# Loading the first input block in full rows and doing its first stage whole, in the prologue of an FFT-and-MLP kernel

## The chip, the cores and the metric

The kernel runs on one core of one Trainium2 chip. The metric is the device time in microseconds (us). Lower is better. A *run* is one timed execution. Most executions of one kernel agree within 0.3%, and that is about the size of the effects here, so medians over five or six runs are given with their range, and ratios with a 95% interval. A *profile* is one execution with a trace. Its *span* runs from the first to the last instruction.

## The reference

```python
# x: (8, 3008, 256) fp32, filt_r and filt_i: (1505, 256), w_in: (256, 2048), w_out: (2048, 256)
X = np.fft.rfft(x, axis=1)
Y = X * (filt_r + 1j * filt_i)[None, :, :]
y = np.fft.irfft(Y, n=3008, axis=1)
h = y.reshape(24064, 256) @ w_in
out = np.maximum(0.01 * h, h) @ w_out
```

The Fourier transform along the sequence is split, 3008 = 94 x 32. Each of the 8 batch elements goes through stage S1 (one 94-point transform as a matmul for each of the 32 values of n2), 32x32 block transposes (T1), stage S2 (32-point transforms), the products with the two filters, the inverse of S2 ("sa"), transposes back (T2), and the inverse of S1 ("sb"). Then comes the MLP, called MoE in the code: 256 to 2048, leaky ReLU, back to 256.

## The kernel before

Batch elements 1 to 7 are transformed beside the MLP, which keeps TensorE busy. Only batch element 0 has nothing to hide behind. Its passage is the *prologue*. It is worked in halves of d (the 256 columns): the first half of x is loaded, then that half's filters, then the second half of x and its filters, and the stages of the two halves are interleaved by hand.

```python
def x_load(b, n0=0, nn=N2, d0=0, dn=D):      # rows of dn values, cast fp32 -> fp16
    ...                                      # issued from GpSimd (POOL)
for i in range(FP):                          # FP = 4, step = 8: the tables of S1
    nc.sync.dma_start(f1_sb[:, ts(i, step), :], f1_d.ap()[i])
nc.sync.dma_start(small_sb[:], small_d.ap())
for hf in range(2):
    for n0 in (0, N2 // 2):
        x_load(0, n0, N2 // 2, hf * DH, DH)  # 16 n2 of 128 columns
    filt_load(fa_sb, filt_r, hf * DH, DH)
    filt_load(fb_sb, filt_i, hf * DH, DH)
# ... (cut)
def first_s1(hf, g, kind, copy):             # 4 n2 of 128 columns: matmuls, one eviction
    ps = bank(kind, 4, DH)
    for j in range(4):
        n2 = 4 * g + j
        nc.tensor.matmul(ps[:, j, :], f1_sb[:N1, n2, :], x_sb[:N1, n2, ts(hf, DH)],
                         start=True, stop=True)
    spread(big[0], 4 * g, ps, copy, hf * DH // 2)

def upper(hf):                               # filters to the other 64 partitions
    for t, cp in ((fa_sb, act), (fb_sb, dve)):
        cp(t[64:P, :, ts(hf, DH)], t[0:64, :, ts(hf, DH)])

def keep_warm(n):                            # n matmuls whose result nobody reads
    ...
for g in range(8):
    first_s1(0, g, two[(g // 2) % 2], (act, dve)[g % 2])
t1_part(0, 0, True)(), t1_part(0, 1, True)()
upper(0)
first_s2(0, 8, 8, True)                      # True: products on POOL, from ACT's copy
first_s2(0, 0, 8, False)                     # False: products on VectorE (DVE)
first_s2(0, 20, 4, True)
first_s2(0, 16, 4, False)
for g in range(8):
    first_s1(1, g, two[g % 4 == 3], dve if g in (3, 5, 7) else act)
x_load(1)
t1_part(0, 2, True)(), t1_part(0, 3, True)()
upper(1)
first_sa(0, 0), first_sa(0, 16)              # inverse of S2, evicted by ScalarE (ACT)
first_s2(1, 8, 8, True)
first_s2(1, 0, 8, False)
# ... w_out load (cut)
first_sa(0, 8), first_sa(0, 20)
first_s2(1, 16, 8, False)
first_sa(1, 0)
first_t2(0), first_t2(1)
first_sa(1, 16), first_sa(1, 8)
first_t2(2), first_t2(3)
keep_warm(5)
for g in range(8):
    first_sb(g, act, two[(g // 2) % 2])
keep_warm(3)
for g in range(8, 16):
    first_sb(g, (act, dve)[g % 2], two[(g // 2) % 2])
```

## Time and profile before

| | kernel before |
|---|---|
| time, median of 3 runs (range) | 785.91 us (785.34 to 786.10) |
| time and span of the profiled execution | 787.67 us and 785.9 us |
| first MoE matmul in that profile | 45.56 us |
| length of the part after it | 740.34 us |

### The profile page before, as it was taken

Reading aid. Unit: us, or ns where it says so; the run is one execution under the profiler, and the core shown is the slowest. Engines: PE = TensorE matmul, PEld = TensorE weight load, DVE = VectorE, ACT = ScalarE, POOL = GpSimd, SP = SyncE. Lnnn points to the kernel's source line nnn. Section 1 sums busy time; section 2 is a strip of 40 time slices with the busy share of each in tenths; the row PEclk is TensorE's granted clock in tenths of the full one; section 3 lists DMA queues with packets and bytes.
Section 4 is the critical chain, followed back from the end, with each engine's and each line's share of the span. In section 5 each row is a group of like instructions: output and inputs, shape, how many; then the busy total and the mean of one; then the engine's idle time right before and its main releaser. Section 6 shows DMA issues by size and latency. Waiting matters only on the chain.

```text
span 785.9 us, 13623 instructions
## 1 busy us (share of the span) xinstructions
PE 763.0 (97%) x5812; PEld 528.6 (67%) x5812; DVE 365.1 (46%) x459; ACT 557.0 (71%) x794; POOL 150.7 (19%) x122
## 2 busy tenths in 40 slices
PE   2799999999999999999999999999999999999998
PEld 1356677666776677866777667776677667676666
DVE  3869760784327652387316754078432765200000
ACT  3686768676687767877687775967668776666664
POOL 5773400240003400052001410024000340000000
PEclk9999999999999999999999999999999999999999
DMA  9943010501032010501014101050100101101111
GB/s 174 214 59 94 28 42 28 122 28 41 28 79 70 28 41 28 119 31 41 28 41 108 41 28 41 28 120 28 42 28 28 41 28 42 41 28 41 41 41 54
DMA packets 42013, 43.39 MB, mean 55 GB/s; under 512 B 14274, under 2 KB 40514, under 8 KB 41282
## 3 DMA queue, kind: packets, MB, share of 16 engines
q0 software_dynamic: 15760, 16.99, 13.2%
q1 hardware_dynamic: 26192, 25.53, 9.3%
q8 instruction: 45, 0.74, 0.4%
q14 instruction: 16, 0.13, 0.1%
HBM read 34.10 MB, written 24.64 MB: 75 GB/s over the span
## 4 chain that ended last, share of the span: by engine, by line
PE 93%; ACT 2%; issue 1%; DVE 0%; ACTq 0%; DVEq 0%
PE po_ps L379 41%; PE ph L365 40%; PE pf L170 3%; PE pf L237 2%; PE pf L210 2%; PE pf L225 2%; PE pf L379 1%; ACT big L181 1%; ACT gt_c L370 1%; PE pf L284 1%; PE ph L260 0%; PE ph L301 0%; DVE fy_h_c L276 0%; PE po_ps L313 0%; PE pf L301 0%
## 5 line engine op out<-in xcount | busy, mean ns | idle before, releaser
L370 ACT ACTIVATE gt_c<-ph 128x1024 f16<-128x1024 f32 x376 | 384.8, 1024 | 194.8 <-PE ph L365 193.8
L365 PE MATMUL ph<-yt,w_in_sb 128*128 128x512 f16 (+7 forms) x1728 | 386.6, 351 | 0.4 <-ACT yt L304 0.2
L379 PE MATMUL po_ps<-w_out_sb,gt_c 128*128 128x256 f16 x2944 | 381.5, 272 | 0.6 <-ACT ost_c_t L386 0.6
L379 PEld LDWEIGHTS <-gt_c 128*128 128x128 f16 x3008 | 290.7, 98 | 86.7 <-issue 1.7
L365 PEld LDWEIGHTS <-w_in_sb 128*128 128x128 f16 x1728 | 163.0, 98 | 95.2 <-issue 1.0
L218 POOL TENSOR_TENSOR y_b_g<-p_b_g,p_b_g 128x512 f16<-128x512 f32 x84 | 106.9, 1273 | 225.5 <-DVE p_b_g L216 225.5
L181 ACT CAST big<-pf 128x512 f16<-128x512 f32 x195 | 111.8, 606 | 11.8 <-PE pf L251 11.7
L193 DVE STREAM_TRANSPOSE big<-big 128x1024 f32<-128x1024 f32 x32 | 55.8, 1846 | 127.1 <-ACT big L181 126.7
L240 DVE CAST yt<-pf 128x376 f16<-128x376 f32 x112 | 56.3, 545 | 85.9 <-PE pf L237 85.9
L214 DVE TENSOR_TENSOR p_b_g<-pf,fa_sb 128x512 f32<-128x512 f32 x84 | 58.1, 692 | 38.0 <-PE pf L210 35.5
L386 ACT COPY ost_c_t<-po_ps 128x256 f32<-128x256 f32 x184 | 69.4, 377 | 6.7 <-PE po_ps L379 5.6
L201 DVE STREAM_TRANSPOSE big<-big 128x1024 f32<-128x1024 f32 x28 | 51.1, 1936 | 34.5 <-ACT big L181 34.5
L215 DVE TENSOR_TENSOR p_b_g<-pf,fb_sb 64x512 f32<-64x512 f32 x84 | 58.2, 693 | 1.1
L216 DVE TENSOR_TENSOR p_b_g<-pf,fb_sb 64x512 f32<-64x512 f32 x84 | 57.4, 683 | 1.1
L132 POOL DMA_DIRECT2D x_sb<-in_x_dram x12 | 8.5, 713 | 256.6 <-PE pf L170 255.5
L237 PEld LDWEIGHTS <-big 128*128 128x128 f16 x448 | 25.7, 98 | 13.2
L170 PE MATMUL pf<-x_sb,f_sb 94*128 94x256 f16 x224 | 33.8, 272 | 0.1
L210 PE MATMUL pf<-big,small_sb 128*128 128x512 f16 x84 | 31.8, 379 | 0.0
L225 PE MATMUL pf<-y_b_g,small_sb 128*128 128x512 f16 x84 | 31.8, 379 | 0.0
L237 PE MATMUL pf<-i_sb,big 128*128 128x94 f16 x448 | 28.7, 206 | 0.0
L170 PEld LDWEIGHTS <-f_sb 94*128 94x128 f16 x224 | 21.0, 97 | 9.5 <-issue 1.3
L347 POOL TENSOR_SCALAR fb_sb<-fb_sb 64x6144 f16<-64x6144 f16 x1 | 15.7, 15742 | 0.4 <-DVE fy_h_c L276 0.4
(45 smaller groups left out, 142.8 us busy)
## 6 DMA issues: line engine op xcount, KB each, us to landing
out_dram<-ost_c_t SPq DMA_DIRECT2D x92, 256.0 KB, 2.1
x_sb<-in_x_dram POOLq DMA_DIRECT2D x6, 1536.0 KB, 11.3
x_sb<-in_x_dram POOLq DMA_DIRECT2D x4, 384.0 KB, 11.0
w_in_sb<-in_moe_w_in_dram POOLq DMA_DIRECT2D x1, 1024.0 KB, 14.9
w_out_sb<-in_moe_w_out_dram POOLq DMA_DIRECT2D x1, 1024.0 KB, 10.2
x_sb<-in_x_dram POOLq DMA_DIRECT2D x1, 1024.0 KB, 9.1
f_sb<-fwd_const SPq DMA_DIRECT2D x4, 192.0 KB, 3.2
fa_sb<-in_filt_r_dram POOLq DMA_DIRECT2D x4, 192.0 KB, 9.8
```

What stands on the lines that cost most here:

```text
L170: nc.tensor.matmul(ps[:, j, :], f1_sb[:N1, n2, :], x_sb[:N1, n2, :], start=True, stop=True)
L181: copy(paired(dst)[:, ds(n0, nn), ds(e0, de)], ps.rearrange("p n (e t) -> p n e t", t=2))
L214: nc.vector.tensor_tensor(p1[:], ps, fa, AL.mult)
L215: nc.vector.tensor_tensor(p2[0:64], ps[64:P], fb[64:P], AL.mult)
L216: nc.vector.tensor_tensor(p2[64:P], ps[0:64], fb[0:64], AL.mult)
L218: nc.gpsimd.tensor_tensor(y1[:], p1[:], p2[:], AL.add)
L237: nc.tensor.matmul(ps[:, j, :], src[:, dt, n2, :], i1_sb[:, n2, :], start=True, stop=True)
L240: copy(yv[:, :, ds(4 * h, 4)], ps.rearrange("p c a -> p a c"))
L365: nc.tensor.matmul(ph[:, j, ds(o, ln)], w_in_sb[:, dt, ts(ct, P)], yts[b % 2][:, dt, ds(lo, ln)], start=(dt == 0), stop=(dt == NDT - 1),)
L370: nc.scalar.activation(gts[ci][:, ds(2 * g, 2), :], ph, AF.Lrelu)
L379: nc.tensor.matmul(po, gts[ci][:, ct, ts(tj, P)], w_out_sb[:, ct, :], start=(ct == 0), stop=(ct == NCT - 1))
L386: nc.scalar.copy(ost[:, tj % 2, :], po)
```

## The change

The intent: load x in long rows, so that the transfer is more efficient; do S1 in one pass, so that no second pass sits in the middle of the prologue; split into halves of d only from T1 on; and put TensorE's work in the order in which its inputs become ready.

```diff
     nc.sync.dma_start(small_sb[:], small_d.ap())
+    for i in range(FP):
+        x_load(0, step * i, step)
     for hf in range(2):
-        for n0 in (0, N2 // 2):
-            x_load(0, n0, N2 // 2, hf * DH, DH)
         filt_load(fa_sb, filt_r, hf * DH, DH)
         filt_load(fb_sb, filt_i, hf * DH, DH)
 ... (cut)
-    def first_s1(hf, g, kind, copy):
-        ps = bank(kind, 4, DH)
-        for j in range(4):
-            n2 = 4 * g + j
-            nc.tensor.matmul(ps[:, j, :], f1_sb[:N1, n2, :], x_sb[:N1, n2, ts(hf, DH)],
+    def first_s1(n0, n, kind, copy):
+        ps = bank(kind, n, D)
+        for j in range(n):
+            nc.tensor.matmul(ps[:, j, :], f1_sb[:N1, n0 + j, :], x_sb[:N1, n0 + j, :],
                              start=True, stop=True)
-        spread(big[0], 4 * g, ps, copy, hf * DH // 2)
+        spread(big[0], n0, ps, copy)
 ... (cut)
-    for g in range(8):
-        first_s1(0, g, two[(g // 2) % 2], (act, dve)[g % 2])
+    for g in range(6):
+        first_s1(4 * g, 4, "ph", (dve, act)[g % 2])
+    for g in range(4):
+        first_s1(24 + 2 * g, 2, two[g == 3], (act, dve)[g % 2])
     t1_part(0, 0, True)(), t1_part(0, 1, True)()
     upper(0)
     first_s2(0, 8, 8, True)
+    x_load(1)
     first_s2(0, 0, 8, False)
+    t1_part(0, 2, True)()
     first_s2(0, 20, 4, True)
     first_s2(0, 16, 4, False)
-    for g in range(8):
-        first_s1(1, g, two[g % 4 == 3], dve if g in (3, 5, 7) else act)
-    x_load(1)
-    t1_part(0, 2, True)(), t1_part(0, 3, True)()
+    t1_part(0, 3, True)()
+    first_sa(0, 0), first_sa(0, 16)
     upper(1)
-    first_sa(0, 0), first_sa(0, 16)
     first_s2(1, 8, 8, True)
+    first_sa(0, 8), first_sa(0, 20)
     first_s2(1, 0, 8, False)
     nc.gpsimd.dma_start(w_out_sb[:], moe_w_out.rearrange("(ct p) d -> p ct d", p=P))
-    first_sa(0, 8), first_sa(0, 20)
     first_s2(1, 16, 8, False)
 ... (cut)
         first_sb(g, act, two[(g // 2) % 2])
-    keep_warm(3)
     for g in range(8, 16):
```

## The prediction

> **What bounds the kernel now.** I read the page first (busy shares, slices, chain), then the windows of the span cut at the first MoE matmul, then the timeline and the waits of the first 46 us, then the DMA view in short windows.
>
> From the page of the kernel before:
>
> ```profile
> PE 763.0 (97%) x5812; PEld 528.6 (67%) x5812; DVE 365.1 (46%) x459; ACT 557.0 (71%) x794; POOL 150.7 (19%) x122
> ...
> PE   2799999999999999999999999999999999999998
> ```
>
> From the windows, cut at 45.56 us (columns: stretch, length, then PE, PEld, DVE, ACT, POOL busy, clock, DMA share, GB/s):
>
> ```profile
> 0.00:45.56 45.56, 26.86 (x236) 16.03 (x237) 27.13 (x31) 26.38 (x42) 32.56 (x31) 0.96 1.27 187
> 45.56:785.90 740.34, 736.12 (x5576) 512.58 (x5575) 337.97 (x429) 530.62 (x752) 118.10 (x92) 1.00 0.17 47
> ```
>
> After 45.56 us TensorE is busy 736.1 of 740.3 us: nothing that the diff touches can shorten that part. Before it no engine is busy for more than 72%; it is a chain of dependent steps. So the time is 740.3 plus the prologue's length, and the change is about the prologue.
>
> The prologue's timeline (start, duration, engine, line, operation; in brackets idle time and what ended it):
>
> ```profile
> 9.59 1.01 PE L251 MATMUL pf<-x_sb,f_sb 94*128 94x128 f16 x8 [9.59 <-DMA x_sb<-in_x_dram]
> ...
> 12.45 1.01 PE L251 MATMUL pf<-x_sb,f_sb 94*128 94x128 f16 x8 [0.99 <-DMA x_sb<-in_x_dram]
> ...
> 15.15 2.37 DVE L193 STREAM_TRANSPOSE big<-big 128x1024 f32<-128x1024 f32 x2
> ...
> 22.46 1.46 PE L251 MATMUL pf<-x_sb,f_sb 94*128 94x128 f16 x12
> ...
> 26.88 2.37 DVE L193 STREAM_TRANSPOSE big<-big 128x1024 f32<-128x1024 f32 x2
> ...
> 34.70 1.22 DVE L276 TENSOR_TENSOR fy_h_c<-ph,fa_sb 128x1024 f16<-128x1024 f32 x1 [1.06 <-PE ph L260]
> ...
> 39.69 2.37 DVE L292 STREAM_TRANSPOSE big<-big 128x1024 f32<-128x1024 f32 x2 [0.35 <-ACT big L285]
> ...
> 45.56 1.28 PE L365 MATMUL ph<-yt,w_in_sb 128*128 128x512 f16 x4 [0.17 <-ACT yt L304]
> ```
>
> The reader is to see three clocks. Loads set the first 12.5 us. From 15.15 to 42.06 VectorE runs an almost closed sequence (27 us with some 4.7 us of gaps), in which the second half of d has its S1 only at 22.46 to 26.1, so that its transpose waits until 26.88. Then ScalarE's twelve copies of the last inverse stage (40.28 to 45.51) carry it to the MoE.
>
> The DMA view of 12 to 16 us (256 B packets, x and filters by halves), and of 27 to 29 us (4 KB packets, the first MoE weight):
>
> ```profile
> DMA packets 2865, 0.72 MB, mean 181 GB/s; under 512 B 2865, under 2 KB 2865, under 8 KB 2865
> ```
>
> ```profile
> DMA packets 100, 0.41 MB, mean 205 GB/s; under 512 B 0, under 2 KB 0, under 8 KB 100
> ```
>
> **What the Trainium skill says.** "DMA: Bandwidth & Descriptors", Specifications, wants at least 512 B per transfer for line rate, and its section on small descriptors names a fixed cost per packet. The trace agrees in direction only: 256 B packets land at 181 GB/s, 4 KB ones at 205, 13% more (both cast from fp32, so twice that is read). The same page, "Issuing engines are not separate DMA queues", says that all queues share 16 engines; the trace agrees, the tables loaded from SP and x from POOL share the 3 to 7 us stretch at 135 to 224 GB/s. "TensorE: Matmul & The Clock Gate", "What's actually happening", says that TensorE idles at 1.2 GHz and goes to 2.4 after a busy free-running window of about 3.4 us. The trace agrees: 512-column matmuls of L284 come every 0.43 us at 31 to 33 us and every 0.215 us after 34.4 us; the granted clock is 0.50 from 30.6 to 34.0 us. The same page gives run-to-run phase as a cause of variation.
>
> **The change part by part.**
>
> *Loads.* Total bytes are equal. First x goes from four loads of 1536 packets to four of 96 packets of 4 KB (8 n2 of 256 values). All of x now precedes all filters. Bytes of the tables: four of 192 KB and one of 96 KB, 885 KB; at 280 GB/s (DMA view, 2 to 3.5 us) and with 350 KB moved by 3.0 us (windows of 1 us: 51 and 299), 1.9 us are left when x starts, near 3.0 us. x: 1573 KB at 205 = 7.7 us. Last byte at 3.0+1.9+7.7 = 12.6, landing some 0.9 later: 13.5 us (estimate). Before, half of d was there at 12.4, so the first transpose does not start earlier: this is the price. First-half filters, 786 KB at 181 = 4.35 us, end at 16.95 and land near 18.9 (lags of about 1.9 us for such packets: the first x load landed at 9.55 when the windows' sum less the tables says 727 KB had moved, 393 of them its own). Before, the last of them was there by about 16.4.
>
> *S1.* 64 matmuls of 128 columns at 0.107 us become 32 of 256 at 0.213 cold: 6.8 us on TensorE either way, all of it under the load now. Evictions: before 16 of 512 columns (ACT 0.59, DVE 0.69), now six of 1024 (ACT 1.02 from L370's row, DVE 1.22 from L276's) and four of 512. Each quarter (1.9 us of arrival) has one DVE and one ACT eviction in parallel, so they keep up. The last quarter: 8 x 0.213 after 13.5 = 15.2, plus 0.1 and a DVE copy of 0.69: first transpose at 16.0 against 15.15. Loss 0.85 us.
>
> *The middle.* From the second half go 3.6 us of TensorE (22.46 to 26.05) and three DVE evictions (2.07 us) between the first multiplications and the second transposes. I add up the new DVE order with measured durations: transposes 16.0 to 18.4; wait for the filter, copy 0.95 until 19.85; S2 on PE 4 x 0.43 from 18.5, so multiplications 20.4 to 22.85 (2.45); third transpose to 24.05 (1.2); the pair of 0.69 to 25.4; fourth transpose to 26.6 (before: 29.25). So 2.65 us are gained here. Then the other engines: ACT's copies of the first half's inverse must wait for 25.4, end at 27.0; ACT copies fa 2.75 to 29.75, evicts 1.1 to 30.85 for POOL, which starts at 30.3 (31.21 before). PE: two S2 matmuls to 27.55, six inverse ones (2.6 us cold, 1.3 warm), two S2 matmuls: DVE's next multiplications start at 31.0 cold or 29.8 warm (31.29 before). So the new PE order takes 2.2 to 3.5 us of the gain back as a DVE gap. Two pairs of multiplications (4.9) end at 35.95 or 34.7; before 37.05. Gain here 1.1 to 2.35.
>
> *The end.* The last inverse matmuls on PE: 8 x 0.215 warm, then five warming ones 1.1, so the last stage starts at 37.6 (warm early) or 38.9 (warm from about 31 to 34 on); before 39.8. Its first eviction comes 0.48 later and the twelve ACT copies take 5.23 as before. Removing the three warming matmuls frees 0.75 us of PE (42.31 to 43.06), of which nearly nothing shows, as ACT copied until 43.39 and had 0.16 us of gap. First MoE matmul: 37.6+0.48+5.25 = 43.3, or 38.9+0.48+5.25 = 44.6. Middle 43.7, as the S1 burst may leave PE warm earlier than I count; against 45.56 a gain of 1.9 us. 740.3 + 43.7 = 784.0.
>
> **The rivals.**
> One: loads. If the filters in second place are what the first S2 products wait for, each us of their delay past 20 us goes through to the end. For it: the filters' share of the queue is unchanged and they move behind 1.57 MB instead of 0.79. Against: by my sum fb's upper copy ends at 19.85 and S2's matmuls at 20.35. If they land 2 us later: 786.
> Two: clock. Without a dense stretch of TensorE between 26 and 34 us, or without the three warming matmuls, the last inverse and the last stage run at half clock: 8 x 0.215 and 5 x 0.215 more, 2.8 us, and the first MoE slots too: 786.5 to 787.5. For it: the phase of the window is free. Against: PE has a closed stretch from 26.7 to 31.
> Three: DVE stays closed. If PE is warm through the middle (S1 at 8 x 0.213 of each 1.9 us is a 90% busy stretch), and the loads land 1 us sooner, DVE's gap shrinks: 781.5 to 782.5.
> Four: the freed prologue is given back in the first MoE slots by a late load. Against: the first MoE weight landed 14 us before use and the next x moves up, as POOL issues it before its second pair instead of after. I give it nearly nothing.
>
> **Range and chances.** My middle is 784.0. Rival three gives the low edge, 781.8; rivals one and two the high edge, 786.5. The prologue would have to lose 16 us of its 45 for "faster by over 2%", and grow by 16 for slower: 1% each. 98% within 2%.
>
> **What would show it right or wrong.** First MoE matmul near 43.7 (43.3 to 44.6), and the rest 740.3 long. Last x quarter at 13.5, first transpose at 16.0, fourth ended at 26.6. A DVE gap of 2 to 3.5 us before the multiplications of the second half, ended by PE. The twelve ACT copies still 5.2 us. Wrong if the first transpose is at 14.5 or 17.5, if filters end DVE's or ACT's waits after 20 us, if L284's matmuls after 35 us come every 0.43 us, or if the part after the prologue changes by over 0.5 us.

## More of the kernel before

The timeline of VectorE in the kernel before shows the second half of the work (start, length, engine, line, operation, output <- input; in brackets the idle time before the first of the group and what ended it):

```profile
29.29 0.96 DVE L308 COPY fb_sb<-fb_sb 64x3072 f16<-64x3072 f16 x1
31.29 1.23 DVE L276 TENSOR_TENSOR fy_h_c<-ph,fa_sb 128x1024 f16<-128x1024 f32 x1 [1.04 <-ACT fx_h_c L268]
...
36.97 2.36 DVE L292 STREAM_TRANSPOSE big<-big 128x1024 f32<-128x1024 f32 x2
```

After the filter copy VectorE waits 1.04 us for ScalarE, then multiplies, and the transposes back start at 36.97.

## The result, and the profile after

| | before | after |
|---|---|---|
| time, median of 6 runs (range) | 785.62 us (784.71 to 786.52) | 786.66 us (785.51 to 789.65) |
| ratio after/before, 95% interval | | 1.0021 (1.0000 to 1.0043) |
| time and span of the profiled execution | 787.67 and 785.9 us | 789.03 and 787.1 us |
| first MoE matmul in it | 45.56 us | 46.75 us |

A ratio is the mean time of one kernel's fast runs over that of the other's of the same rounds, so it is not quite the ratio of the medians. I predicted 784.0 us, at most 786.5. The change did not save 1.9 us; it cost about 1 us by the medians and 1.7 us by the means. The prediction was wrong.

Four views of the kernel after. First the page's busy times, to be held against those of before:

```profile
PE 764.4 (97%) x5777; PEld 526.2 (67%) x5777; DVE 366.2 (47%) x457; ACT 556.1 (71%) x790; POOL 148.8 (19%) x122
```

TensorE is busy 1.4 us longer, VectorE 1.1 us, ScalarE 0.9 us less: on this page the change is not to be seen, as it lies in who waits for whom. Then the windows, cut at the first MoE matmul, with the columns of the prediction:

```profile
0.00:46.75 46.75, 28.31 (x201) 13.62 (x202) 28.24 (x29) 25.51 (x38) 30.99 (x31) 0.96 1.09 182
46.75:787.10 740.35, 736.13 (x5576) 512.59 (x5575) 337.95 (x429) 530.61 (x752) 117.80 (x92) 1.00 0.17 47
```

The second part is 740.35 us against 740.34. Everything happens in the prologue, as predicted, and the difference of the two spans, 1.2 us, is the difference of the two prologues. The timeline of the prologue after:

```profile
9.03 1.86 PE L250 MATMUL ph<-x_sb,f_sb 94*128 94x256 f16 x8 [9.03 <-DMA x_sb<-in_x_dram]
...
18.21 2.37 DVE L193 STREAM_TRANSPOSE big<-big 128x1024 f32<-128x1024 f32 x2
...
27.31 1.23 DVE L193 STREAM_TRANSPOSE big<-big 128x1024 f32<-128x1024 f32 x1
...
32.31 1.22 DVE L275 TENSOR_TENSOR fy_h_c<-ph,fa_sb 128x1024 f16<-128x1024 f32 x1 [1.68 <-ACT fx_h_c L267]
...
40.61 2.37 DVE L291 STREAM_TRANSPOSE big<-big 128x1024 f32<-128x1024 f32 x2 [1.40 <-ACT big L284]
...
46.75 1.28 PE L364 MATMUL ph<-yt,w_in_sb 128*128 128x512 f16 x4 [0.17 <-ACT yt L303]
```

The reader is to see that the first transpose moved from 15.15 to 18.21, and that the fourth ends at 28.54 against 29.25 before: the whole loss of 3.06 us is made good in the middle, and 0.71 more. It is lost again after that. VectorE has a gap of 1.68 us before the second half's products, ended by ScalarE (before, that gap was 1.04), and one of 1.40 us before the last transposes (before, 0.35).

The second gap falls into a window of half clock. The windows of the kernel after around it, each 3.41 us long and cut at or one such length before a change in the record of the granted clock (the last three numbers are clock, DMA share and GB/s):

```profile
33.79:37.20 3.41, 1.70 (x8) 0.41 (x7) 3.41 (x4) 1.58 (x3) 3.41 (x4) 1.00 0.86 183
37.20:40.62 3.42, 3.42 (x10) 1.21 (x9) 2.02 (x3) 2.42 (x4) 3.34 (x2) 0.50 0.54 65
40.62:44.03 3.41, 3.32 (x79) 2.64 (x79) 2.36 (x2) 2.20 (x7) 3.41 (x1) 1.00 1.38 187
```

In the first window TensorE was busy for half of the time (1.70 us); in the next one the record grants half the clock, and ten matmuls took all of 37.20 to 40.62. The kernel before had the same in its profile (0.50 from 30.6 to 34.0, after a window with 2.08 us busy). How busy a window has to be does not come out of these traces: in "before, early S1" (below) one with only 1.78 us busy, 22.20 to 25.61, was followed by full clock. So neither of the two profiles that I had was of an undisturbed execution, and a comparison of the two mixes the change with luck.

### The profile page after: what moved, and what is told of

Same layout as the page of the kernel before. It is cut to its first block, busy times and chain, and to the rows that moved or that the text cites. A ratio compares the mean times of both kernels' runs of the same rounds, so it can differ in the third digit from the quotient of the medians.

```text
span 787.1 us, 13542 instructions
## 1 busy us (share of the span) xinstructions
PE 764.4 (97%) x5777; PEld 526.2 (67%) x5777; DVE 366.2 (47%) x457; ACT 556.1 (71%) x790; POOL 148.8 (19%) x122
## 4 chain that ended last, share of the span: by engine, by line
PE 94%; ACT 2%; DVE 1%; DMA 1%; issue 1%; POOL 0%; ACTq 0%; DVEq 0%; POOLq 0%
PE po_ps L378 41%; PE ph L364 40%; PE pf L170 3%; PE pf L237 2%; PE pf L225 2%; PE pf L210 2%; DMA x_sb<-in_x_dram 1%; PE pf L378 1%; ACT big L181 1%; DVE fy_h_c L275 1%; PE pf L283 1%; ACT gt_c L369 1%; PE ph L250 0%; ACT fa_sb L307 0%; DVE big L193 0%
## 5 line engine op out<-in xcount | busy, mean ns | idle before, releaser
L181 ACT CAST big<-pf 128x512 f16<-128x512 f32 x190 | 109.0, 607 | 0.0
L132 POOL DMA_DIRECT2D x_sb<-in_x_dram x12 | 6.6, 553 | 256.6 <-PE pf L170 255.8
L250 PE MATMUL ph<-x_sb,f_sb 94*128 94x256 f16 x26 | 6.2, 412 | 10.1 <-DMA x_sb<-in_x_dram 9.6
```

Of the source, the lines that this page charges most:

```text
L181: copy(paired(dst)[:, ds(n0, nn), ds(e0, de)], ps.rearrange("p n (e t) -> p n e t", t=2))
```

## The experiments

**How they are read.** Of every profile I note three numbers: the start of the first transpose ("T1 starts"), the first MoE matmul, and their difference, the *rest* of the prologue. The first is set by loads and S1, the rest by the chain of engines. The last column says whether a window of half clock fell into the rest of the prologue after the first release.

| kernel | last x needed lands | T1 starts | first MoE | rest | half-clock window |
|---|---|---|---|---|---|
| before, as profiled | 12.41 | 15.15 | 45.56 | 30.41 | yes |
| before with filling matmuls | 10.41 | 13.15 | 42.42 | 29.27 | no |
| after, as profiled | 15.47 | 18.21 | 46.75 | 28.54 | yes |
| after again | 14.76 | 17.61 | 44.02 | 26.41 | no |
| load alone | 14.40 | 16.39 | 45.64 | 29.25 | no |
| after, order back | 14.40 | 17.31 | 43.56 | 26.25 | no |
| after, warming three back | 14.28 | 17.13 | 43.91 | 26.78 | no |
| after, tables in line | 13.69 | 16.44 | 44.82 | 28.38 | yes |
| after with filling matmuls | 14.45 | 17.19 | 43.61 | 26.42 | no |
| before, early S1 | 10.59 | 13.34 | 40.97 | 27.63 | no |
| the same, filled | 10.53 | 13.28 | 40.91 | 27.63 | no |
| after, best order | 15.30 | 18.05 | 43.27 | 25.22 | no |
| the same, tables in line | 13.64 | 16.39 | 41.60 | 25.21 | no |
| halves of x first | 10.68 | 13.42 | 42.77 | 29.35 | no |

Two profiles of one structure without a half-clock window repeat the rest to 0.02 us: 29.27 and 29.25 (S1 by halves with either load), 26.41 and 26.42, 27.63 and 27.63, 25.22 and 25.21. The landing of x is what varies between executions. Timed runs carry both kinds of luck; the table separates them. Each row is a single profile. All kernels were correct. All experiments are of five rounds, and those of one call share the runs of the kernel before.

### First call: parts of the change

**Load alone.** The kernel before with only the loads of the change. S1 and everything else stay by halves.

```diff
+    for i in range(FP):
+        x_load(0, step * i, step)
     for hf in range(2):
-        for n0 in (0, N2 // 2):
-            x_load(0, n0, N2 // 2, hf * DH, DH)
         filt_load(fa_sb, filt_r, hf * DH, DH)
```

> The kernel before with the new load alone (full rows by quarters of n2, all of x ahead of all filters), S1 still by halves of d. Theory L (the late x is what eats the gain): the last quarter lands near 15.5 us instead of 12.4, the first transpose starts near 17 to 18 us instead of 15.15, filters land 3.4 us later, and about 2 us of it reach the end: +1.5 to +2.5 us against before. Rival O (the load is harmless, the new order of TensorE and ScalarE work costs): within 0.5 us of before.

Measured: 788.01 us (787.69 to 789.8) against 786.36 of before; ratio 1.0028 (1.0016 to 1.0040). The load alone is a loss, and the interval excludes 1. The loss of 1.65 us in the medians is as expected; T1 starts somewhat sooner than the 17 to 18 us expected. VectorE's timeline in this run:

```profile
16.39 2.37 DVE L193 STREAM_TRANSPOSE big<-big 128x1024 f32<-128x1024 f32 x2
...
28.12 2.37 DVE L193 STREAM_TRANSPOSE big<-big 128x1024 f32<-128x1024 f32 x2
```

T1 starts 3.24 us later than in the undisturbed kernel before (13.15), and the first MoE matmul comes 3.22 us later (45.64 and 42.42). What the load costs goes through to the end undiminished. The rest of the change then takes 45.64 to 44.02 in the undisturbed profile of the kernel after: a gain of 1.62. So +3.22 - 1.62 = +1.60.

**Order back.** The kernel after, with the second half's S2 ahead of the two inverse groups again.

```diff
-    first_sa(0, 8), first_sa(0, 20)
     first_s2(1, 0, 8, False)
+    first_sa(0, 8), first_sa(0, 20)
```

> The changed kernel with one pair of lines exchanged: S2 of the second half's first 8 columns stands again before the two inverse groups of the first half's last columns. Theory O: VectorE's 1.7 us gap before the second half's products shrinks by some 1.7 us, and since the last S2 pair waits for ScalarE anyway, 0.5 to 1 us reach the end (-0.5 to -1 against the changed kernel). Theory L alone: 0 to -0.3, as the chain is then held by ScalarE's copy of the filter and its evictions.

Measured: 785.84 us (785.4 to 786.52); ratio 0.9997 (0.9986 to 1.0009). By the medians that looks like 0.8 us won over the kernel after, but all five runs had a mean clock of at least 0.999, and of the kernel after two in six did not. The profile gives the true size: the rest is 26.25 instead of 26.41, so 0.16 us. VectorE's gap before the products shrinks only from 1.23 to 1.07 us, and it is still ScalarE's filter copy that ends it:

```profile
30.80 1.23 DVE L275 TENSOR_TENSOR fy_h_c<-ph,fa_sb 128x1024 f16<-128x1024 f32 x1 [1.07 <-ACT fa_sb L307]
```

TensorE's order was not what made that gap, contrary to the prediction.

**Warming three back.** The kernel after with the three warming matmuls that the change takes away.

```diff
         first_sb(g, act, two[(g // 2) % 2])
+    keep_warm(3)
     for g in range(8, 16):
```

> The changed kernel with the three warming matmuls put back between the halves of the last stage. Theory C (their loss lets TensorE's clock fall): -0.5 to -1.5 us in those executions where the clock is low. Theory L, and the profile's reading that ScalarE's twelve copies bound that stage: +0 to +0.5 us, as 0.65 us of TensorE time come back and mostly hide.

Measured: 787.80 us (786.1 to 789.09); ratio 1.0024 (1.0010 to 1.0037). Three of six runs still fell to a mean clock of 0.998 and had spans of 786.7 to 787.0, against 784.2 to 785.0 for the other three. So the removal of the three is not what exposes the kernel to the half clock. The rest is 26.78, 0.37 longer than without them: their removal is a true gain of 0.37 us, where I had counted "nearly nothing".

**Tables in line.** The kernel after, with the second to fourth quarter of S1's tables issued from POOL, each just ahead of the quarter of x that needs it, instead of from SP beside all of them.

```diff
+    nc.sync.dma_start(f1_sb[:, ts(0, step), :], f1_d.ap()[0])
     for i in range(FP):
-        nc.sync.dma_start(f1_sb[:, ts(i, step), :], f1_d.ap()[i])
-    nc.sync.dma_start(small_sb[:], small_d.ap())
-    for i in range(FP):
+        if i:
+            nc.gpsimd.dma_start(f1_sb[:, ts(i, step), :], f1_d.ap()[i])
         x_load(0, step * i, step)
+    nc.gpsimd.dma_start(small_sb[:], small_d.ap())
```

> The changed kernel with table quarters 2 to 4 and the small matrices issued from the same software queue, each ahead of its x quarter, so the two queues no longer alternate on the 16 engines. Theory L in the form 'alternation of the two queues delays x0 and slows the whole stretch to 180 GB/s': x0 lands near 7 us instead of 9.0, the last near 13.5 to 14.5 instead of 15.5, the first transpose 1 to 2 us earlier, total -1 to -2 us against the changed kernel. Rival: the engines are simply short of bandwidth for tables and x together: last landing unchanged within 0.3 us, total the same.

Measured: 785.83 us (785.35 to 787.43); ratio 1.0003 (0.9990 to 1.0015). Two of the five runs were at a mean clock of 0.998, the profiled one among them. The last quarter of x lands at 13.69 and T1 starts at 16.44, 0.7 us earlier than the earliest of the six profiles of the kernel after and its variants with the tables on SP (17.13). The time is 0.83 us below that of the kernel after, where 1 to 2 us had been expected; with two executions at the lower clock, and no run of the kernel after beside it, that stays unsettled. The order of issue is taken up again below.

### Second call: clock and order

**After again**, unchanged, for an undisturbed profile beside the next ones on one chip.

> The changed kernel itself once more, on the same chip and in the same rounds as its variants. Theory L with C: +0.5 to +2 us against before, two groups of times, near 785.8 and near 789. Its profile, if at full clock, should show the first MoE matmul near 43.5 to 44.5 us, not 46.75; the landing of the last x quarter between 14.3 and 15.5.

Measured: 786.56 us (786.13 to 789.21); ratio 1.0023 (1.0006 to 1.0040), which repeats the result. Two of six runs had a clock of 0.996 and spans of 786.1 and 787.1; the other four had 784.2 to 784.7, and times of 786.13 to 786.74. The profile is one of the four. The four runs of the kernel before at a clock of 1.0 in this call took 784.45 to 784.86. Full clock against full clock, the change costs some 1.7 us in this call, more than the medians of all runs say. (In the other two calls the runs of before at a clock of 1.0 go up to 785.68 and 786.81.)

**Before with filling matmuls.** Dummy matmuls where TensorE would else idle in the middle of the prologue.

```diff
     first_sa(0, 0), first_sa(0, 16)
+    keep_warm(4)
     first_s2(1, 8, 8, True)
 ... (cut)
     first_sa(1, 0)
+    keep_warm(4)
     first_t2(0), first_t2(1)
```

> The kernel before with eight dummy matmuls (four in the 1.3 us wait ahead of the second half's S2, four after the second half's first inverse groups). Theory C says that the profile shown of before was itself a low-clock execution (0.50 from 30.6 to 34.0): this one should never show that, its times should sit at the lower end of before's, 784.7 to 786, mean 0.3 to 1 us below before. Rival: the 0.50 stretch costs before nothing, as its chain then ran on VectorE: no change within 0.3 us.

Measured: 784.74 us (784.47 to 785.11); ratio 0.9990 (0.9978 to 1.0002). All five runs had a clock of 1.0 and spans of 782.7 to 783.3. Of the eleven runs of the plain kernel before in the same call, seven had 0.997 or 0.998 with spans of 783.8 to 785.9, and four had 1.0 with spans of 782.7 to 783.1, the same as with the filling. In these five runs the filling costs nothing, and none shows the lower clock. The interval includes 1, so the gain of 0.8 us in the mean is not secured; the narrow range is plain to see.

With this pair I have two matched executions. Their windows, cut at the start of T1, at the end of the fourth transpose, at the start of T2 and at the first MoE matmul. First the kernel before, filled:

```profile
0.00:13.15 13.15, 3.73 (x32) 3.41 (x32) 3.74 (x6) 4.33 (x7) 9.54 (x16) 1.00 1.31 173
13.15:27.27 14.12, 9.22 (x48) 5.24 (x49) 11.49 (x12) 9.67 (x11) 9.04 (x10) 1.00 1.59 220
27.27:33.83 6.56, 6.14 (x21) 2.14 (x21) 5.49 (x6) 5.09 (x10) 4.62 (x5) 1.00 1.11 232
33.83:42.42 8.59, 8.20 (x144) 5.77 (x143) 6.38 (x9) 7.13 (x16) 8.51 (x2) 1.00 1.17 178
```

The kernel after again, in the same windows:

```profile
0.00:17.61 17.61, 7.30 (x32) 4.37 (x32) 6.03 (x7) 6.01 (x8) 9.04 (x18) 1.00 1.09 184
17.61:27.94 10.33, 5.62 (x12) 1.44 (x12) 9.15 (x9) 5.49 (x7) 6.38 (x7) 1.00 1.39 230
27.94:35.80 7.86, 5.62 (x17) 1.71 (x18) 6.61 (x6) 6.79 (x9) 5.30 (x6) 1.00 1.07 226
35.80:44.02 8.22, 7.66 (x140) 5.61 (x140) 6.44 (x9) 6.95 (x16) 8.14 (x3) 1.00 0.92 119
```

Stage by stage the change is +4.46, -3.79, +1.30 and -0.37, in sum +1.60. The second row is the intended gain: 12 matmuls instead of 48 between T1 and the fourth transpose. It is smaller than what the first row loses. The third row is a new loss. VectorE's timelines show where it is, first in the kernel before, filled, then in the kernel after again:

```profile
27.30 0.95 DVE L308 COPY fb_sb<-fb_sb 64x3072 f16<-64x3072 f16 x1
29.29 1.22 DVE L276 TENSOR_TENSOR fy_h_c<-ph,fa_sb 128x1024 f16<-128x1024 f32 x1 [1.04 <-ACT fx_h_c L268]
```

```profile
27.96 2.07 DVE L307 COPY fb_sb<-fb_sb 64x3072 f16<-64x3072 f16 x1
31.26 1.22 DVE L275 TENSOR_TENSOR fy_h_c<-ph,fa_sb 128x1024 f16<-128x1024 f32 x1 [1.23 <-ACT fa_sb L307]
```

ScalarE's copy of `fa` in the same two executions, in the same order:

```profile
24.29 2.75 ACT L308 COPY fa_sb<-fa_sb 64x3072 f16<-64x3072 f16 x1
```

```profile
28.32 2.75 ACT L307 COPY fa_sb<-fa_sb 64x3072 f16<-64x3072 f16 x1
```

And POOL in the kernel after again:

```profile
28.05 1.16 POOL L270 TENSOR_TENSOR fy_h_c<-fx_h_c,fb_sb 128x512 f16<-128x512 f32 x1
```

VectorE's products of the second half read the filter `fa` on all 128 partitions, so they need ScalarE's copy. The change puts the evictions of two inverse groups ahead of that copy, and they in turn wait for the first half's products; in the filled kernel before, the copy started at 24.29, 2.98 us before the fourth transpose ended, here at 28.32, 0.38 us after it, and it ends at 31.07. From the end of the fourth transpose to the products it was 2.02 us before (copy 0.95, wait 1.04) and is 3.32 now. The wait is only 0.19 us longer, as VectorE's own copy of `fb` takes 2.07 instead of 0.95 us beside POOL's product; but a shorter copy would only have waited longer, since ScalarE's copy ends at 31.07. The Trainium skill, page "SBUF — State Buffer", section "SBUF: two separate sides", says that the port pair that VectorE and GpSimd share is an exclusive lock, held for a whole instruction. It says so of VectorE's two-port modes; whether this copy ran in one, no run shows. The trace agrees in size: POOL's product is on until 29.21, and 29.21 plus 0.95 is 30.16, where the copy ended at 30.03.

**After with filling matmuls.** The same cure for the kernel after.

```diff
     first_s2(1, 16, 8, False)
+    keep_warm(2)
     first_sa(1, 0)
+    keep_warm(4)
     first_t2(0), first_t2(1)
```

> The changed kernel with six dummy matmuls in TensorE's waits late in the prologue (two after the last S2, four after the second half's first inverse groups). Theory C (about a third of the changed kernel's executions have their clock window fall on that thin stretch, drop to half clock there and lose some 3 us): no executions 2 us or more above the fastest, the median 0 to 1 us and the mean 1 us lower than the changed kernel run beside it, and the profile without a 0.5 stretch after 25 us. Rival (the spread has another cause, such as the landing time of x): spread as wide as before, mean unchanged.

Measured: 786.12 us (785.89 to 787.6); ratio 1.0012 (0.9999 to 1.0025). No run fell below 0.999, and the profile's rest is 26.42, as in the undisturbed kernel after. The slowest two runs have spans of 785.1 and 785.5 at a clock of 0.999 and 1.0; I cannot say what set them, as they have no trace. So the half clock costs the change something in a third of its executions (four of twelve), but near full clock it is still not shown to be faster than the kernel before.

**Before, early S1.** If S1 in the middle is the trouble and waiting for all of x is the price, S1 of the second half can be taken out of VectorE's way without a new load. Four of its groups run on TensorE ahead of the last S2 group, evicted by ScalarE, which had idle time there.

```diff
     first_s2(0, 20, 4, True)
+    for g in range(4):
+        first_s1(1, g, "pf", act)
     first_s2(0, 16, 4, False)
-    for g in range(8):
-        first_s1(1, g, two[g % 4 == 3], dve if g in (3, 5, 7) else act)
+    for g in range(4, 8):
+        first_s1(1, g, two[g == 4], (dve, act)[g % 2])
```

> The kernel before with only one idea of the change: order by readiness. Loads as before; four of the second half's eight S1 groups go ahead of the last S2 pair of the first half, where x has landed and ScalarE is idle, and ScalarE evicts six of the eight. If the second half's late S1 is what the change was right to attack, the third transpose starts near 25.4 us instead of 26.9 and -1 to -1.5 us reach the end, without the price of the late x (theory L). Rival: ScalarE's copy of the filter and its evictions hold the chain, gain under 0.4 us.

Measured: 783.92 us (783.05 to 784.88) against 785.57; ratio 0.9981 (0.9967 to 0.9994). The interval excludes 1. The timeline:

```profile
23.45 2.37 DVE L193 STREAM_TRANSPOSE big<-big 128x1024 f32<-128x1024 f32 x2
...
40.97 1.28 PE L367 MATMUL ph<-yt,w_in_sb 128*128 128x512 f16 x4 [0.17 <-ACT yt L304]
```

The second pair of transposes starts at 23.45, and the first MoE matmul comes 1.45 us earlier than in the filled kernel before. The change's gain in the middle can be had, in part, without its price at the start. Three of the six runs were still at 0.998 and 1.5 us longer.

### Third call: the parts put together

**The same, filled**, with three and four dummy matmuls that read tables already loaded.

```diff
+    def fill(n):
+        for _ in range(n):
+            nc.tensor.matmul(po_ps.rearrange("p a d -> p (a d)"), small_sb[:R1, 0, :],
+                             f1_sb[:].rearrange("p a d -> p (a d)")[:, 0:512],
+                             start=True, stop=True)
 ... (cut)
     first_sa(0, 0), first_sa(0, 16)
+    fill(3)
     first_s2(1, 8, 8, True)
 ... (cut)
     first_sa(1, 0)
+    fill(4)
     first_t2(0), first_t2(1)
```

> The kernel before with the early S1 groups and seven dummy matmuls (three ahead of the second half's S2, four after its first inverse groups). If early S1 is worth 1.45 us and the low-clock executions another 0.8 on average: 782.9 to 783.6, no execution over 784, -2 to -2.6 us against before. Rival (the two gains overlap): as the early S1 alone, 784.0 in the mean with two groups 1.5 us apart.

Measured: 783.56 us (783.26 to 785.17) against 785.77; ratio 0.9981 (0.9968 to 0.9993). It beats the kernel before, but two of five runs were at a clock of 0.999 and 784.65 and 785.17 us: the filling does not always hold, so that part of the expectation failed. The ratio is no better than without it.

**After, best order.** The kernel after with ScalarE's filter copy of the second half right behind its last product copy of the first, the S2 order of "order back", and filling.

```diff
     first_s2(0, 20, 4, True)
+    act(fa_sb[64:P, :, ts(1, DH)], fa_sb[0:64, :, ts(1, DH)])
     first_s2(0, 16, 4, False)
     t1_part(0, 3, True)()
     first_sa(0, 0), first_sa(0, 16)
-    upper(1)
+    dve(fb_sb[64:P, :, ts(1, DH)], fb_sb[0:64, :, ts(1, DH)])
     first_s2(1, 8, 8, True)
-    first_sa(0, 8), first_sa(0, 20)
     first_s2(1, 0, 8, False)
+    first_sa(0, 8), first_sa(0, 20)
 ... (cut)
     first_sa(1, 0)
+    fill(4)
```

> The changed kernel with its middle put right: ScalarE's copy of the second half of the first filter where ScalarE waits (before the last S2 pair of the first half), S2 ahead of the two inverse groups, four dummy matmuls. If the late x is what the change pays (theory L), the first transpose still starts at 17.2 to 17.6 us and the first MoE matmul comes at 42.5 to 43: 784.6 to 785.2, at best equal to a full-clock execution of before. Theory O (the order was the fault): VectorE's gap before the second half's products goes to under 0.5 us and the time falls below 784.

Measured: 784.73 us (784.12 to 785.85); ratio 0.9993 (0.9981 to 1.0006). The rest is 25.22, 1.19 us less than in the kernel after, and VectorE has no gap between its copy and the products. The three edits together are worth that much; filling alone changed nothing (26.42), the S2 order alone gave 0.16, so about 1.0 us is left for ScalarE's copy, if the parts add up (that edit was not run alone). The gap is gone and the time is still not below 784, as it would be if the order had been the main fault; T1 is late as in the kernel after. All five runs had a clock of 1.0. The profiled one had its x late (15.30), so its span of 783.6 is among the longer ones.

**The same, tables in line.** Added: the loads of "tables in line".

> The same with the tables in the same queue as x. Last x near 13.7, first transpose 16.4, everything 0.7 us earlier than in the last kernel: 783.9 to 784.5. Rival: the filters' landing near 18.3, unchanged, then holds VectorE and only 0.2 us comes through.

Measured: 783.93 us (783.8 to 784.21); ratio 0.9979 (0.9966 to 0.9993). This kernel beats the kernel before in the same rounds, and the kernel after by comparison across calls; its range of 0.4 us is the narrowest of all. Against the last kernel the median gains 0.8 us. VectorE's timeline:

```profile
16.39 2.37 DVE L194 STREAM_TRANSPOSE big<-big 128x1024 f32<-128x1024 f32 x2
...
26.75 2.07 DVE L338 COPY fb_sb<-fb_sb 64x3072 f16<-64x3072 f16 x1
28.84 1.22 DVE L276 TENSOR_TENSOR fy_h_c<-ph,fa_sb 128x1024 f16<-128x1024 f32 x1
...
33.38 2.36 DVE L292 STREAM_TRANSPOSE big<-big 128x1024 f32<-128x1024 f32 x2
```

Copy, products and transposes follow without a gap. The copy still takes 2.07 us, but with nothing to wait for after it the products start 2.13 us after the fourth transpose ends, against 2.02 in the filled kernel before.

The DMA view of 3 to 10 us tells what the tables in line do. The kernel after, then this one:

```profile
DMA packets 480, 1.25 MB, mean 178 GB/s; under 512 B 67, under 2 KB 76, under 8 KB 480
```

```profile
DMA packets 436, 1.52 MB, mean 217 GB/s; under 512 B 65, under 2 KB 65, under 8 KB 436
```

In the kernel after, the tables come on the SP queue beside x: their quarters land at 3.26, 5.10, 9.16 and 11.50 us, the last two 0.17 us after a quarter of x (8.99 and 11.33). In the kernel before, they landed at 3.34, 3.85, 5.24 and 7.56. I read from this that the two queues were served in turn, and that with long rows in x's queue the tables get through later. That reading is argued, not shown. Nor is 178 GB/s the price of it: the other six profiles with this load and the tables on SP moved 193 to 211 GB/s in the same stretch, and 178 belongs to the execution whose x landed last. Shown is that with the tables in line the last x lands at 13.64 and 13.69 in two profiles (217 and 213 GB/s), against 14.28 to 15.47 in seven. A simpler cause was not tested apart: the small matrices, 96 KB, land before the last quarter of x in the kernel after (14.18, then 15.47), and after it here (13.64, then 13.90). At 205 GB/s that is 0.5 us (an estimate), most of the smallest difference.

**Halves of x first.** Is waiting for full rows the whole price? Here x comes by halves of d as before, but both halves ahead of all filters, with S1 by halves, all of it before S2, and the best order after it.

```diff
-    for i in range(FP):
-        x_load(0, step * i, step)
+    for hf in range(2):
+        for n0 in (0, N2 // 2):
+            x_load(0, n0, N2 // 2, hf * DH, DH)
 ... (S1 by halves again; cut)
     t1_part(0, 0, True)(), t1_part(0, 1, True)()
+    for g in range(8):
+        first_s1(1, g, two[(g // 2) % 2], (act, dve)[g % 2])
+    t1_part(0, 2, True)(), t1_part(0, 3, True)()
     upper(0)
```

> Both halves of x still ahead of all filters and all of S1 still before S2, but x in halves of d and S1 by halves: the first transpose needs only the first half of x. If waiting for full rows is the price (theory L in its narrow form): first transpose near 13.2, the third near 18, first MoE matmul 41 to 42, 783 to 784 us, about 1 us better than the last kernel but one. Rival: putting x ahead of the filters is the price whatever S1 does: the filters land near 19 us, S2's products start at 20.2 to 21 us, no better than 784.6.

Measured: 785.02 us (784.74 to 786.05); ratio 0.9995 (0.9983 to 1.0008). I had hoped for 783 to 784, so it missed by 1 us. VectorE's timeline:

```profile
13.42 2.37 DVE L194 STREAM_TRANSPOSE big<-big 128x1024 f32<-128x1024 f32 x2
...
20.84 1.78 DVE L309 COPY fb_sb<-fb_sb 64x3072 f16<-64x3072 f16 x1
22.66 1.22 DVE L277 TENSOR_TENSOR fy_h_c<-ph,fa_sb 128x1024 f16<-128x1024 f32 x1
```

T1 starts at 13.42, but the products only at 22.66, where "early S1" has them at 17.83. Between lie four evictions, the second half's transposes and a filter copy, and VectorE goes from one to the next with hardly a gap. So neither x (its second half landed at 15.05) nor the filters, which now come behind all of x (the last of the first half landed at 19.36, before VectorE's copy at 20.84), kept it waiting there. T1 is early, as with halves of x before, so waiting for full rows is what delays T1. But up to the second half's products VectorE needs 16.59 us from T1, against 14.51 in "early S1": its two filter copies take 1.78 and 2.52 us instead of 0.96 and 0.95, and it has four evictions on the way instead of two. Why the copies are that long here was not tested; POOL's products ran beside both.

## Why the prediction was wrong

Its working gives 43.7 us of prologue in the middle; the undisturbed kernel after has 44.02. That it came so close is partly luck: T1 came 1.61 us later than predicted, and from T1 to the first MoE matmul it took 26.41 us instead of 27.7. Most durations were right. The steps that failed are what the sum was compared with (points 1 and 2), the landing of x (3), and what ends VectorE's wait in the middle (5).

1. **"The time is 740.3 plus the prologue's length": failed, by 1.9 us.** That sum is a span. The time of the same execution is longer, 787.67 against 785.9 before and 789.03 against 787.1 after. With it the prediction would have read about 785.9, and the range would have held the result. The sum looked right because the profile's span, 785.9, was the same number as the median time. Nor is the difference the same for all kernels: 1.72 to 1.85 us where S1 is by halves ("load alone" included), 1.82 to 2.20 where it is whole. So about 0.25 us of the change's cost (the means are 1.77 and 2.03) lies outside the spans, where no trace shows what it is.
2. **"Against 45.56 a gain of 1.9 us": failed, by 2.1 us.** 45.56 was the prologue of a slow execution. The typical one of before follows from the median: 785.62 less 1.77 less 740.34 is 43.5. Against that, 43.7 is no gain. In that profile the first x landed at 12.41 instead of 10.41 to 10.59, and a window ran at half clock. I had seen the second, and counted it into the base as if each execution had it. The profile alone told it: its own time stood 1.8 us above the median.
3. **"Loss 0.85 us" for the first transpose: mis-sized.** It was +4.46 between matched executions, 13.15 and 17.61. Of that, 0.85 was predicted and 2.0 are point 2 (15.15 in the slow execution). The other 1.61 are in my own value of 16.0. The last quarter of x lands at 14.28 to 15.47 in seven profiles, not at 13.5. I took 280 GB/s for the rest of the tables and then 205 for x, while tables and x together came at 178 to 211 GB/s between 3 and 10 us in these profiles; with 205 for both, the same sum gives 14.2 (an estimate). From landing to T1 it takes 2.7 to 2.9 us with S1 whole, against my 2.5.
4. **The middle, T1 to the end of the fourth transpose: right.** Predicted 10.6, measured 10.33; the gain of 3.79 is there.
5. **"A DVE gap of 2 to 3.5 us, ended by PE": wrong in its cause.** There is a gap, but of 1.23 us, and ScalarE's filter copy ends it; the kernel before had one of 1.04. I had counted that copy for POOL alone. The order-back run shows TensorE's part to be 0.16 us; the best-order run shows the copy's place, the order and the filling together to be 1.19. From the fourth transpose to T2 I predicted 8.1 to 9.35; 7.86 was measured. Before it was 6.56, so the change still loses 1.30 here.
6. **The end: nearly right.** 8.6 predicted, 8.22 measured. Taking out the three warming matmuls was worth 0.37, not "nearly nothing".
7. **Rival one (filters): did not happen.** They landed at 19.75 instead of 18.9, still before the first transposes ended at 20.58. **Rival two (clock): happened** in two of six, two of six and, with the warming three back, three of six executions, which were 2 to 3 us longer in the mean (read from each run's mean clock; only the profiled ones show the window). But the kernel before has it as well, for 1.4 us in the mean in seven of eleven runs of one call, so little of the difference of the medians comes from it: the runs of the change at a clock of 0.999 or 1.0, 785.51 to 786.74, are not faster than those of before at 1.0 (784.45 to 786.81) either. **Rival three** (781.5 to 782.5; by that sum a span) is what the last kernels reach, by other means. **Rival four (a late load in the MoE): did not happen**; that part is 740.35 us against 740.34.

One reading in the prediction is off without consequence: the gaps in VectorE's sequence from 15.15 to 42.06 come to 5.2 us, not 4.7.

What stays open: the 0.25 us outside the spans, which windows bring the half clock, why landings of the same loads differ by over 1 us from one execution to the next, why the shown execution of the kernel before had x 2 us late, and the two runs at a clock of 0.999 in the filled "early S1".

## What to carry to other kernels

Before a profile is used as the base of an estimate, hold its own time against the median of the runs, its span against its time, and its clock and first landings against a second profile: here these three together were worth more than the whole effect. A transfer in longer rows gains little if the first consumer then has to wait for all of it, as T1 did here; the moment at which the first engine can start counts, and so does what else is loaded ahead of it. When work is put earlier on one engine, look at what then stands behind it there: a copy which two engines need must not come after evictions that wait.

## What the Trainium skill lacked or had wrong

- "TensorE: Matmul & The Clock Gate", section "What's actually happening", gives an idle window as what brings the half clock back. Here windows of 3.41 us with TensorE busy for 1.70, 1.85 and 2.08 us went before one of half clock in three profiles, and one with 1.78 us busy did not in a fourth.
- No page that I found gives the size of what a moving operand in short strided pieces costs a matmul; "SBUF — State Buffer" and "Advanced Engine Details and Errata" name a penalty without a figure. In "after again", at full clock, the S2 matmuls of 512 columns (pieces of 4 bytes, 128 bytes apart) started 0.412 to 0.415 us apart, and the inverse ones, of as many columns, 0.215 us apart. That the pieces are the cause was not tested.
- No page that I found says that a profile can show full clock before the first release, a time in which "TensorE: Matmul & The Clock Gate" has the throttled state as its default. In these traces the record begins only there (22.2 to 30.4 us), and the profile shows 1.00 for the time before, in which the contiguous 512-column matmuls came 0.426 us apart.
- "DMA: Bandwidth & Descriptors", Specifications, wants at least 512 bytes per transfer for line rate. Here packets of 256 bytes landed at 181 GB/s and those of 4 KB, of another tensor, at 205, only 13% more; 4 KB packets of x beside the tables of another queue came with them to 178 to 211.
- No page that I found gives the spread of landings: the same last quarter of x landed at 14.28 to 15.47 us in seven profiles.
